# A convolution and a squared-ReLU MLP on one core: the first superblock of tokens in a set order, the biases moved to the second

## The chip, the cores and the metric

The kernel runs on one core of a Trainium2 chip. The metric is the device time of one execution in microseconds (us), as the median of several runs. Engines go by the profile's names: PE is TensorE, PEld its weight loads, DVE is VectorE, ACT is ScalarE, POOL is GpSimd, SP is SyncE, which here only issues DMAs.

## What is computed

Each of 8 sequences of 4096 tokens (192 channels) is convolved causally with 7 softmax-normalised taps per head. Then every token goes through an MLP of width 2048 with a squared ReLU:

```python
w = softmax(weight)                                  # 8 heads x 7 taps
out = np.einsum('hk,bskhg->bshg', w, x_unf)          # causal convolution
h = x @ w_in                                         # 192 -> 2048
r = np.maximum(h, 0.0)
g = s * (r * r) + b
return (g @ w_out).astype(np.float32)                # 2048 -> 192
```

The constant b contributes b times the column sums of w_out, one number for each output channel. That is the bias of which this document speaks.

## The kernel before, in words

**Tiling.** Everything is transposed: channels lie on the 128 partitions, tokens along the free axis. The 32768 tokens are 32 superblocks of 1024 (index n), each of two blocks of 512 (j = 0, 1). The 16 slices of the hidden width are taken as 8 pairs (p). One step (n, j, p) computes two slices of h for 512 tokens (`first`, 18 matmuls of 64 rows on L465, two at a time on the two halves of the array), squares them, and two steps later (LAG = 2) adds their share to the output accumulators (`second` on L529, or `second_whole` on L501 to L508 for n = 0). The numbers are kept as a high and a low part: qh and ql of the squares, W's two parts of the weights, sA and tB of the convolved tokens.

**Halves.** A matmul of 64 rows reads its tokens from either half of the partitions, so each of sA (channels 0 to 127) and tB (channels 128 to 191) has a copy with the halves exchanged, wA and wB. `swap` makes it with two DMAs on SP's queue (L156 and L157 of before). A step's matmuls read sA first, then tB and wB, then wA. The tB and wB of a superblock hold both of its blocks, in one tile each.

**Who does what in a step.** ACT: Relu of h out of PSUM (L474), the square (L475). DVE: the rounded copy qh (L481) and the remainder ql (L482). For n = 0 the copy qh is on ACT (L479).

**The next tokens.** While superblock n runs, DVE convolves superblock n+1. `Tokens.steps` is a generator, and each of its yields is one part: 7 taps for accA of block 0, 2 for splitting it, 7 taps for accB, 1 for hiB, 2 for the two halves of tB, 1 for the swap of tB into wB (it yields the mark "block 0"), then 9 for block 1 of accA: 29 parts. `convolve(k)` takes k parts behind DVE's last instruction. For n > 0 it is called with 2 at the pairs p < 7 of both blocks: 28 parts a superblock. `ready` calls `finish` ahead of a block's first step: `finish("block 0")` takes parts until it meets that mark; where the mark has already gone by, it meets none and takes all that is left.

**The weights.** They arrive as 64-bit floats. `Widen` makes the two parts of a pair's weights: an Abs on ACT (`magnitudes`), three DVE operations and two ACT copies into W (`top`), six DVE operations (`rest`, L288 to L295). In the first superblock, pair p+2 is widened while pair p runs; `column_sums` adds the weights up from step 8 on, and `biases` multiplies the sums by b on PE at the superblock's last pair.

**What sets the order.** Each engine executes in program order. `head()` pins its own order on four engines; behind it the order comes from a scheduler that takes what is ready by priority, with `issue_after` as the only hints. Superblock 0 goes by pairs, both blocks of a pair one after the other; the others go block by block.

Of the kernel before, what the change touches and what calls it, by code (L numbers as in the profile page):

```python
# [9 lines left out]
F32 = mybir.dt.float32  # L10
F32R = mybir.dt.float32r
# [12 lines left out]

CONV0, CONVN = 5, 2

SUM0 = 8

# [8 lines left out]
def conv_attention_then_squared_relu_mlp(  # L37
# [42 lines left out]

    @contextmanager
    def behind(*engines):


        with ExitStack() as stack:
            for e in engines:
                last = next(i for i in reversed(nc.cur_bb.bb.instructions) if i.engine == e.engine)
                stack.enter_context(tc.issue_after(last))
            yield

# [19 lines left out]
    class Tokens:  # L110
        def __init__(self, n):
            self.n = n
            self.sA, self.wA = {}, {}
            self.todo = self.steps() if n else iter(())

        def load(self):
# [54 lines left out]
        def split_B(self, acc):  # L171
# [13 lines left out]
            self.swap(self.wB, self.tB)  # L185

        def split_tensor(self, acc, hi):
# [58 lines left out]
    class Widen:  # L246
# [21 lines left out]
        def top(self):  # L268
            t, top = self.t, words[self.p][:, self.lo : self.hi, 1]
            nc.vector.tensor_scalar(  # L270
                t.bitcast(F32), t.bitcast(F32), TOP_MIN, TOP_MAX, op0=ALU.max, op1=ALU.min
            )
# [8 lines left out]
            for hi, _, t in self.parts(t.bitcast(F32)):  # L281
                nc.scalar.copy(hi, t)

        def rest(self):
# [12 lines left out]
        def all(self):  # L297
            self.magnitudes()
            self.top()
            self.rest()  # L300

# [40 lines left out]
    def head():  # L342
# [5 lines left out]
        for _ in range(WARM):  # L348
# [3 lines left out]
            )  # L352
        w0, w0out, w1 = Widen(0, 0, CI), Widen(0, CI, CT), Widen(1, 0, CT)

# [19 lines left out]
        next(split)  # L374
        w0.top()
        next(split)
        fetch(2)
        w0.rest()
        w0out.magnitudes()
        tB = one.tB = xs.tile([P, 2, BLK], F32R, name="tB")  # L380
# [6 lines left out]
        lo(tB[bottom, 0, :], top)  # L387
        lo(wB[top, 0, :], top)
        w0out.top()
        w1.magnitudes()  # L390
        w0out.rest()
        sA = one.sA[1] = xs.tile([P, 2, BLK], F32R, name="sA", bufs=3)
# [6 lines left out]
        one.swap(wB[:, 1, :], tB[:, 1, :])  # L399
        w1.top()  # L400
        w1.rest()

    ENGINES = (nc.vector, nc.scalar, nc.tensor, nc.sync)
    with in_order(*ENGINES):
        head()
    headed = {
        e: next(i for i in reversed(nc.cur_bb.bb.instructions) if i.engine == e.engine)
        for e in ENGINES
    }

    @contextmanager
    def behind_head(*engines):
        with ExitStack() as stack:
            for e in engines:
                stack.enter_context(tc.issue_after(headed[e]))
            yield

# [26 lines left out]

    bias = const.tile([P, 2], F32, name="bias")

    def biases():


        pb = ps_h.tile([P, 2, BLK], F32, name="h")[:, 0, 0:2]  # L450
        for i, cols in enumerate((sumA[:, 0, 0:P], sumB[:, 0:P])):
            nc.tensor.matmul(pb[:, i : i + 1], cols, bb, start=True, stop=True)
        nc.scalar.copy(bias, pb)


    def first(n, j, p):
# [12 lines left out]
        for at in (0, 2, 1):  # L469
            both(0, 1, at, at == 0, False)  # L470
            both(0, 2, at, False, False)
            both(1, 1, at, False, at == 1)
        q = act.tile([P, 2, BLK], F32, name="q")
        nc.scalar.activation(q, h, AF.Relu)  # L474
        nc.scalar.activation(q, q, AF.Square)  # L475
        qh = qs.tile([P, 2, BLK], F32R, name="qh")
        ql = qs.tile([P, 2, BLK], F32R, name="ql")
        if n == 0:
            nc.scalar.copy(qh, q)  # L479
        else:  # L480
            nc.vector.tensor_copy(qh, q)  # L481
        nc.vector.tensor_tensor(ql, q, qh.bitcast(F32), op=ALU.subtract)  # L482
# [9 lines left out]
    def second_whole(n, j, p, qh, ql):  # L492


        if (j, p) == (0, NPAIR - 1):
            biases()
        a1, a2 = accumulators(n, j, p)
# [11 lines left out]
        if p == NPAIR - 1:  # L509
            t0 = n * SUP + j * BLK  # L510
            oA = outs.tile([P, BLK], F32, name="oA")
            nc.scalar.activation(oA, a1, AF.Identity, scale=sb, bias=bias[:, 0:1])
            nc.sync.dma_start(outT[0:P, t0 : t0 + BLK], oA)
            oC = outs.tile([DB, BLK], F32, name="oC", bufs=1)
            nc.scalar.activation(oC, a2[DB:P, :], AF.Identity, scale=sb[DB:P], bias=bias[DB:P, 1:2])
            oB = outs.tile([P, BLK], F32, name="oB")
            nc.vector.scalar_tensor_tensor(
                oB[0:DB], a2[0:DB, :], sb[0:DB], oC, op0=ALU.mult, op1=ALU.add
            )
            nc.sync.dma_start(outT[P:D, t0 : t0 + BLK], oB[0:DB])  # L520
            del acc[n, j]
# [47 lines left out]
    def last(t0, accs):  # L569
# [7 lines left out]
        for k, o in ((1, oB), (3, oC)):  # L577
            nc.vector.scalar_tensor_tensor(
                o, accs[k][0:DB], sb[0:DB], o, op0=ALU.mult, op1=ALU.add
            )  # L580
        nc.gpsimd.tensor_tensor(oB, oB, oC, op=ALU.add)
        nc.sync.dma_start(outT[P:D, t0 : t0 + BLK], oB)
# [12 lines left out]


    steps = [(0, j, p) for p in range(NPAIR) for j in range(2)]
    START = len(steps)
    steps += [(n, j, p) for n in range(1, NSUP) for j in range(2) for p in range(NPAIR)]
    queue = []  # L600
# [3 lines left out]
    def convolve(k):  # L604

        done = object()
        with behind(nc.vector):
            while k and coming[0] in tok:
                if next(tok[coming[0]].todo, done) is done:
                    coming[0] += 1  # L610
                else:
                    k -= 1

    def upkeep(at, n, j, p):

        if n == 0 and j == 1 and p + 2 < NPAIR:
            with behind_head(*ENGINES):
                if p + 3 < NPAIR:
                    fetch(p + 3)
                Widen(p + 2, 0, CT).all()  # L620
                if p == 0:
                    start_tokens(1)
        if 0 <= at - SUM0 < NPAIR - 1:
            with behind(nc.vector):
                column_sums(at - SUM0 + 1)
        if n == 0:
            if at >= CONV0:
                convolve(CONVN)
        elif p < NPAIR - 1:
            if j == 0 and p == 0:  # L630
                with behind_head(nc.sync):
                    start_tokens(n + 1)
            convolve(2)

    def ready(n, j, p):
        if p == 0 and n > 0:
            tok[n].finish("block 0" if j == 0 else None)
        if n > 0 and j == 1 and p == 0:
            tok.pop(n - 1)

    for at in range(0, START, 2):
        batch = steps[at : at + 2]
        for step in batch:
            ready(*step)
        for k, step in enumerate(batch):
            with behind_head(nc.scalar, nc.tensor):
                queue.append((*step, *first(*step)))
            upkeep(at + k, *step)
        while len(queue) > LAG:
            second_whole(*queue.pop(0))  # L650
    for at, step in enumerate(steps[START:], START):
        ready(*step)
        queue.append((*step, *first(*step)))
        upkeep(at, *step)
# [42 lines left out]
```

## Time and profile before

| | us |
|---|---|
| median of 3 runs (lowest, highest) | 2316.5 (2315.3, 2318.49) |
| the profiled execution | 2314.63 |
| its span, first to last instruction | 2312.8 |
| PE busy / DVE / ACT / POOL | 2295.4 / 1754.7 / 1289.0 / 306.0 |

The profile page gives the busy time of each engine. The timeline view lists instructions as start, duration, engine, line, tiles and, in brackets, the idle time ahead and what ended it. The windows view sums a stretch: length, then the busy time and number of instructions of PE, PEld, DVE, ACT and POOL, the granted TensorE clock, the busy share of the DMA engines, GB/s. The issue view gives the time from a DMA's issue to its landing. A matmul of 512 columns is drawn 0.39 us long while the next starts 0.23 us behind it, so PE's busy time hides short pauses.

### The profile page before, as it was taken

To read this page: it belongs to the slowest core of one execution; us is meant where nothing else is said; L and a number is where in the kernel's file an instruction comes from. 1 tells how busy PE (TensorE), PEld (TensorE's weight loads), DVE (VectorE), ACT (ScalarE), POOL (GpSimd) and SP (SyncE) were. 2 spreads that over 40 slices of the span, in tenths; PEclk is the share of its full clock that TensorE was granted. 3 is DMA by queue.
4 is the path that set the end of the run, shared out by engine and by line. 5 is a ranking of instruction groups with operands and counts; after the bars stand their busy time and mean duration, and the time that the engine had idled before them with its cause. 6 is when DMAs were issued, how large, how long until landed. Compare 5 with 4: busy or idle time off the path is not lost.

```text
span 2312.8 us, 45113 instructions
## 1 busy us (share of the span) xinstructions
PE 2295.4 (99%) x19334; PEld 1829.4 (79%) x19334; DVE 1754.7 (76%) x1993; ACT 1289.0 (56%) x1408; POOL 306.0 (13%) x207
## 2 busy tenths in 40 slices
PE   8999999999999999999999999999999999999998
PEld 5688888888888888888888888888888888888887
DVE  8877777777777777777777777777777777777764
ACT  7755555555555555554555555555555555555554
POOL 0001011011110110111111101101111011011111
PEclk9999999999999999999999999999999999999999
DMA  5112121111111111111112111111112121111110
GB/s 174 55 33 60 37 60 51 52 42 44 54 51 51 42 52 46 54 55 50 46 42 56 51 51 42 49 49 51 51 43 59 38 60 52 51 42 41 43 38 17
DMA packets 46521, 117.77 MB, mean 51 GB/s; under 512 B 8240, under 2 KB 8496, under 8 KB 46320
## 3 DMA queue, kind: packets, MB, share of 16 engines
q1 hardware_dynamic: 45808, 114.49, 17.9%
q8 instruction: 151, 2.47, 0.5%
q10 hardware_dynamic: 512, 0.40, 0.1%
q14 instruction: 50, 0.41, 0.1%
HBM read 31.63 MB, written 25.17 MB: 25 GB/s over the span
## 4 chain that ended last, share of the span: by engine, by line
PE 78%; issue 16%; DVE 2%; POOL 2%; DMA 1%; ACT 1%; POOLq 0%; DVEq 0%; ACTq 0%
PE acc L529 40%; PE h L465 37%; POOL oB L559 1%; DMA oC<-oB 1%; POOL oC L565 1%; PE acc L218 1%; DVE ql L482 1%; DVE t L277 0%; DVE c L289 0%; DVE W L293 0%; ACT q L474 0%; DVE W L295 0%; PE acc L501 0%; ACT q L475 0%; DMA tap<-in_taps 0%
## 5 line engine op out<-in xcount | busy, mean ns | idle before, releaser
L474 ACT ACTIVATE q<-h 128x1024 f32<-128x1024 f32 x512 | 526.4, 1028 | 719.3 <-PE h L465 716.2
L481 DVE CAST qh<-q 128x1024 fp32r<-128x1024 f32 x496 | 373.3, 753 | 451.0 <-ACT q L475 447.5
L482 DVE TENSOR_TENSOR ql<-q,qh 128x1024 fp32r<-128x1024 f32 x512 | 654.5, 1278 | 60.1 <-ACT qh L479 6.6
L529 PE MATMUL acc<-qh,W 64*128 64x512 f32 x3968 | 623.3, 392 | 0.0
L475 ACT ACTIVATE q<-q 128x1024 f32<-128x1024 f32 x512 | 544.4, 1063 | 16.1
L465 PE MATMUL h<-sA,W 64*128 64x512 f32 x3072 | 442.7, 393 | 6.8 <-ACT q L474 6.8
L529 PEld LDWEIGHTS acc<-qh,W 64*128 64x128 f32 x3968 | 371.7, 184 | 91.2
L465 PE MATMUL h<-wA,W 64*128 64x512 f32 x3072 | 442.5, 392 | 0.0
L465 PE MATMUL h<-wB,W 64*128 64x512 f32 x1536 | 440.4, 392 | 1.9 <-DVE accA L148 1.9
L465 PE MATMUL h<-tB,W 64*128 64x512 f32 x1536 | 440.1, 392 | 0.0
L529 PE MATMUL acc<-qh,WB 64*128 64x512 f32 x1984 | 391.8, 392 | 0.0
L529 PE MATMUL acc<-ql,WB 64*128 64x512 f32 x1984 | 391.8, 392 | 0.0
L529 PE MATMUL acc<-ql,W 64*128 64x512 f32 x1984 | 391.8, 392 | 0.0
L465 PEld LDWEIGHTS h<-sA,W 64*128 64x128 f32 x3072 | 286.7, 184 | 81.4 <-ACT q L474 9.3
L148 DVE SCALAR_TENSOR_TENSOR accA<-xA,tap,accA 128x512 f32<-128x512 f32 x378 | 340.8, 902 | 6.8
L465 PEld LDWEIGHTS h<-wA,W 64*128 64x128 f32 x3072 | 288.8, 184 | 70.7
L465 PEld LDWEIGHTS h<-wB,W 64*128 64x128 f32 x1536 | 282.4, 184 | 49.6 <-DMA wB<-tB 2.8
L559 POOL TENSOR_TENSOR oB<-oB,oB 128x512 f32<-128x512 f32 x61 | 115.4, 1891 | 1486.9 <-ACT oB L558 1486.9
L465 PEld LDWEIGHTS h<-tB,W 64*128 64x128 f32 x1536 | 282.4, 184 | 24.0
L529 PEld LDWEIGHTS acc<-ql,WB 64*128 64x128 f32 x1984 | 185.9, 184 | 45.6
L529 PEld LDWEIGHTS acc<-ql,W 64*128 64x128 f32 x1984 | 185.8, 184 | 45.6
L529 PEld LDWEIGHTS acc<-qh,WB 64*128 64x128 f32 x1984 | 185.8, 184 | 45.6
(95 smaller groups left out, 1019.9 us busy)
## 6 DMA issues: line engine op xcount, KB each, us to landing
wA<-sA SPq DMA_DIRECT2D x128, 256.0 KB, 3.7
outT<-oA SPq DMA_DIRECT2D x63, 256.0 KB, 2.0
wB<-tB SPq DMA_DIRECT2D x62, 256.0 KB, 3.4
xA<-in_xT SPq DMA_DIRECT2D x24, 515.0 KB, 3.4
oC<-oB SPq DMA_DIRECT2D x61, 128.0 KB, 2.2
outT<-oC SPq DMA_DIRECT2D x61, 128.0 KB, 2.3
xB<-in_xT SPq DMA_DIRECT2D x56, 129.5 KB, 2.7
words<-in_w SPq DMA_DIRECT2D x7, 768.0 KB, 6.4
```

What stands on the lines that cost most here:

```text
L148: nc.vector.scalar_tensor_tensor(acc, src, w[:, k : k + 1], acc, op0=ALU.mult, op1=ALU.add)
L218: nc.tensor.matmul(acc, diag[:, k, :], x[:, k : k + BLK], start=k == 0, stop=k == K - 1)
L465: nc.tensor.matmul(h[:, i, :], w_in(w, p, chunk[0], rows), chunk[part], start=start, stop=stop)
L474: nc.scalar.activation(q, h, AF.Relu)
L475: nc.scalar.activation(q, q, AF.Square)
L481: nc.vector.tensor_copy(qh, q)
L482: nc.vector.tensor_tensor(ql, q, qh.bitcast(F32), op=ALU.subtract)
L529: nc.tensor.matmul(accs[to + 2 * i], w(f, r), q[r, f % 2, :], start=start, stop=stop)
L559: nc.gpsimd.tensor_tensor(o[1], o[1], o[3], op=ALU.add)
L565: nc.gpsimd.tensor_tensor(oC, oC, o[1][0:DB], op=ALU.add)
```

## The change

`head()` widens pair 1 before the output weights of pair 0 and leaves two steps, `his` and `rest`, to be called apart. Superblock 0 becomes a loop over `pair(p)` in which DVE, ACT and PE are pinned to the order of the code. The parts of superblock 1's convolution in each pair are a table, CONV: three numbers for three places in the pair. For n = 1 alone, ACT makes the copies of the accB split and writes block 0's wB itself, so that only block 1's wB needs a DMA. `finish` is written anew. `column_sums` and `biases` go to the pairs of (1, 0); the outputs of superblock 0 are made without the bias, and POOL adds it behind them. The very last output's sum moves from POOL to DVE.

```diff
-CONV0, CONVN = 5, 2
-SUM0 = 8
+CONV = ((0, 0, 0),) + ((0, 0, 1),) * 5 + ((0, 1, 3), (4, 2, 2))
...
+        def split_B_at_once(self, acc):
...
+            nc.scalar.copy(hiB, acc)
+            for j in range(2):
+                r = slice(j * DB, (j + 1) * DB)
+                places = (self.tB, self.wB) if j == 0 else (self.tB,)
+                for k, to in enumerate(places):
+                    nc.scalar.copy(to[k * DB :][0:DB, j, :], hiB[r, :].bitcast(F32))
+                for k, to in enumerate(places):
+                    nc.vector.tensor_tensor(
+                        to[(1 - k) * DB :][0:DB, j, :], acc[r, :], hiB[r, :].bitcast(F32),
+                        op=ALU.subtract,
+                    )
+                yield "block 0" if j == 0 else None
+            self.swap(self.wB[:, 1, :], self.tB[:, 1, :])
...
-                    yield from self.split_B(acc)
-                    yield "block 0"
+                    if self.n == 1:
+                        yield from self.split_B_at_once(acc)
+                    else:
+                        yield from self.split_B(acc)
+                        yield "block 0"
...
-        def finish(self, upto=None):
-            for at in self.todo:
-                if upto and at == upto:
-                    break
+        def part(self):
+
+            at = next(self.todo, False)
+            if at == "block 0":
+                self.begun = True
+            return at is not False
+
+        def finish(self, block):
+            while not (block == 0 and self.begun) and self.part():
+                pass
...
+        pb = ps_h.tile([P, 2, BLK], F32, name="h")
+        for k, cols in enumerate((sumA[:, 0, 0:P], sumB[:, 0:P])):
+            for i in range(2):
+                r = slice(i * HB, (i + 1) * HB)
+                nc.tensor.matmul(pb[:, i, k : k + 1], cols[r], bb[r], start=True, stop=True)
+        nc.scalar.copy(bias[:, 0:2], pb[:, 0, 0:2])
+        nc.vector.tensor_tensor(bias[:, 0:2], bias[:, 0:2], pb[:, 1, 0:2], op=ALU.add)
+        nc.vector.tensor_copy(bias[0:DB, 2:3], bias[DB:P, 1:2])
+        for o, to, k in unbiased:
+            rows = slice(0, o.shape[0])
+            nc.gpsimd.tensor_scalar(o, o, bias[rows, k : k + 1], None, op0=ALU.add)
+            nc.sync.dma_start(to, o)
...
-        nc.gpsimd.tensor_tensor(oB, oB, oC, op=ALU.add)
+        nc.vector.tensor_tensor(oB, oB, oC, op=ALU.add)
...
+    def pair(p):
+
+        ha, hb = first(0, 0, p), first(0, 1, p)
+        if 0 < p < NPAIR - 1:
+            wide[p + 1].rest()
+        convolve(CONV[p][0])
+        qa = squares(ha, nc.scalar.copy)
+        if p == 0:
+            wide[2].top()
+        elif p + 2 < NPAIR:
+            wide[p + 2].magnitudes()
+        queue.append((0, 0, p, *lows(*qa)))
+        if 0 < p and p + 2 < NPAIR:
+            wide[p + 2].top()
+        convolve(CONV[p][1])
+        qb = squares(hb, nc.scalar.copy)
+        if p + 2 < NPAIR:
+            wide[p + 2].his()
+        queue.append((0, 1, p, *lows(*qb)))
+        convolve(CONV[p][2])
+        while len(queue) > (LAG if p < NPAIR - 1 else LAG - 1):
+            second_whole(*queue.pop(0))
...
+    for n, j, p in steps:
+        if p == 0:
+            tok[n].finish(j)
...
+        if (n, j) == (1, 0):
+            if p < NPAIR - 1:
+                with behind(nc.vector):
+                    column_sums(p + 1)
+                convolve(2 - p % 2)
+            else:
+                biases()
         elif p < NPAIR - 1:
...
+            convolve(3 if n == 1 else 2)
```

The order of DVE in the first superblock, one pair of it. A line that ends in W_85 is a weight's last operation, ql is the remainder of a block's squares, accA the convolution of superblock 1. Before:

```order
L270 TENSOR_SCALAR t_740<-t_740 128x768
L274 TENSOR_SCALAR t_740<-t_740 128x768
L277 SCALAR_TENSOR_TENSOR t_740<-words_641,t_740 128x768
L482 TENSOR_TENSOR ql_512<-q_508,qh_511 128x1024
L148 SCALAR_TENSOR_TENSOR accA_466<-xA_301,tap_87,accA_466 128x512
L288 TENSOR_SCALAR c_747<-t_740 128x768
L148 SCALAR_TENSOR_TENSOR accA_466<-xA_301,tap_87,accA_466 128x512
L289 SCALAR_TENSOR_TENSOR c_747<-words_641,c_747 128x768
L148 SCALAR_TENSOR_TENSOR accA_466<-xA_301,tap_87,accA_466 128x512
L482 TENSOR_TENSOR ql_540<-q_536,qh_539 128x1024
```

And now, for one pair from its `rest` to its second ql:

```order
L325 TENSOR_SCALAR c_698<-t_623 128x768
L326 SCALAR_TENSOR_TENSOR c_698<-words_482,c_698 128x768
L330 TENSOR_TENSOR W_85<-t_623,W_85 128x640
L330 TENSOR_TENSOR WB_86<-t_623,WB_86 128x2x64
L332 TENSOR_TENSOR W_85<-W_85,c_698 128x640
L332 TENSOR_TENSOR WB_86<-WB_86,c_698 128x2x64
L518 TENSOR_TENSOR ql_712<-q_705,qh_708 128x1024
L305 TENSOR_SCALAR t_710<-t_710 128x768
L309 TENSOR_SCALAR t_710<-t_710 128x768
L312 SCALAR_TENSOR_TENSOR t_710<-words_571,t_710 128x768
L518 TENSOR_TENSOR ql_724<-q_717,qh_720 128x1024
L155 SCALAR_TENSOR_TENSOR accA_367<-xA_237,tap_87,accA_367 128x512
```

The taps, which lay between the parts of a weight, now lie once a pair behind the second ql.

The second place is DVE where tB of superblock 6 is made, late in superblock 5 (hiB is the rounded accB, and each row of tB is half a block's split). Before:

```order
L176 CAST hiB_4733<-accB_4493 128x512
L180 CAST tB_4731<-accB_4493 64x512
L181 TENSOR_TENSOR tB_4731<-accB_4493,hiB_4733 64x512
L481 CAST qh_4794<-q_4791 128x1024
L482 TENSOR_TENSOR ql_4795<-q_4791,qh_4794 128x1024
L180 CAST tB_4731<-accB_4493 64x512
L181 TENSOR_TENSOR tB_4731<-accB_4493,hiB_4733 64x512
L481 CAST qh_4824<-q_4821 128x1024
L482 TENSOR_TENSOR ql_4825<-q_4821,qh_4824 128x1024
L146 TENSOR_SCALAR accA_4828<-xA_4271,tap_87 128x512
```

Now:

```order
L183 CAST hiB_4946<-accB_4794 128x512
L513 CAST qh_4990<-q_4987 128x1024
L518 TENSOR_TENSOR ql_4992<-q_4987,qh_4990 128x1024
L187 CAST tB_4944<-accB_4794 64x512
L188 TENSOR_TENSOR tB_4944<-accB_4794,hiB_4946 64x512
L187 CAST tB_4944<-accB_4794 64x512
L188 TENSOR_TENSOR tB_4944<-accB_4794,hiB_4946 64x512
L513 CAST qh_5040<-q_5037 128x1024
L518 TENSOR_TENSOR ql_5042<-q_5037,qh_5040 128x1024
L513 CAST qh_5093<-q_5090 128x1024
```

Before, tB is done five blocks of squares ahead of superblock 6's first (qh and ql of the steps 3 to 7 of block 1 follow, the taps of block 1 between them). Now it follows the squares q_4987 of step (5, 1, 6); q_5037 are those of (5, 1, 7), and q_5090 already come from the h that reads this tB. On PE that h (h_5071) stands two steps behind the h of q_4987:

```order
L498 MATMUL h_5071<-sA_4727,W_85 128x512 x6
L498 MATMUL h_5071<-tB_4944,W_85 128x512
L498 MATMUL h_5071<-wB_4945,W_85 128x512 x2
L498 MATMUL h_5071<-tB_4944,W_85 128x512 x2
L498 MATMUL h_5071<-wB_4945,W_85 128x512
L498 MATMUL h_5071<-wA_4728,W_85 128x512 x6
```

PE's own order there is as before; what moved is DVE's making of tB, and with it the swap into wB_4945.

More of the change, by code (lines that the diff above doesn't have):

```diff
@@ L79, in conv_attention_then_squared_relu_mlp, with last_of, context @@
     ps_o = ctx.enter_context(tc.tile_pool(name="ps_o", bufs=2, space=bass.MemoryType.PSUM))
-    @contextmanager
-    def behind(*engines):
[L85 to L89, printed above, removed]
+    def last_of(*engines):
+        traced = nc.cur_bb.bb.instructions
+        last = [next(i for i in reversed(traced) if i.engine == e.engine) for e in engines]
+        @contextmanager
+        def context():
+            with ExitStack() as stack:
+                for i in last:
+                    stack.enter_context(tc.issue_after(i))
+                yield
+        return context
+    def behind(*engines):
+        return last_of(*engines)()
     @contextmanager
@@ L185, in split_B @@
             self.swap(self.wB, self.tB)
+        def split_B_at_once(self, acc):
+            self.tB = xs.tile([P, 2, BLK], F32R, name="tB")
+            self.wB = xs.tile([P, 2, BLK], F32R, name="wB")
+            hiB = xs.tile([P, BLK], F32R, name="hiB", bufs=1)
+            nc.scalar.copy(hiB, acc)
[11 more added lines that the diff above has]
+            self.swap(self.wB[:, 1, :], self.tB[:, 1, :])
         def split_tensor(self, acc, hi):
@@ L279, in top, with his @@
             )
-            for hi, _, t in self.parts(t.bitcast(F32)):
+        def his(self):
+            for hi, _, t in self.parts(self.t.bitcast(F32)):
                 nc.scalar.copy(hi, t)
@@ L295, in rest @@
                 nc.vector.tensor_tensor(lo, lo.bitcast(F32), f, op=ALU.add)
[L297 to L300, printed above, removed]
     w_words = weights64.bitcast(I32)
@@ L375, in head @@
         w0.top()
+        w0.his()
         next(split)
         fetch(2)
+        w1.magnitudes()
         w0.rest()
-        w0out.magnitudes()
+        w1.top()
         tB = one.tB = xs.tile([P, 2, BLK], F32R, name="tB")
@@ L388, in head @@
         lo(wB[top, 0, :], top)
+        w0out.magnitudes()
+        w1.his()
         w0out.top()
-        w1.magnitudes()
-        w0out.rest()
+        w1.rest()
         sA = one.sA[1] = xs.tile([P, 2, BLK], F32R, name="sA", bufs=3)
@@ L399, in head @@
         one.swap(wB[:, 1, :], tB[:, 1, :])
[L400 to L416, printed above, removed]
+        w0out.his()
+        w0out.rest()
+        wide[2].magnitudes()
+    wide = {p: Widen(p, 0, CT) for p in range(1, NPAIR)}
     sumA, sumB = None, None
@@ L443, in column_sums @@
             nc.vector.tensor_tensor(b[:, 0:DB], b[:, 0:DB], b[:, DB:P], op=ALU.add)
-    bias = const.tile([P, 2], F32, name="bias")
+    bias = const.tile([P, 3], F32, name="bias")
+    unbiased = []
     def biases():
[L450 to L453, printed above, removed]
+        pb = ps_h.tile([P, 2, BLK], F32, name="h")
[10 more added lines that the diff above has]
+            nc.sync.dma_start(to, o)
     def first(n, j, p):
@@ L472, in first, with squares @@
             both(1, 1, at, False, at == 1)
+        return h
+    def squares(h, cast):
         q = act.tile([P, 2, BLK], F32, name="q")
@@ L476, in first, with lows @@
         qh = qs.tile([P, 2, BLK], F32R, name="qh")
+        cast(qh, q)
+        return q, qh
+    def lows(q, qh):
         ql = qs.tile([P, 2, BLK], F32R, name="ql")
[L478 to L481, printed above, removed]
         nc.vector.tensor_tensor(ql, q, qh.bitcast(F32), op=ALU.subtract)
@@ L604, in convolve @@
     def convolve(k):
-        done = object()
         with behind(nc.vector):
             while k and coming[0] in tok:
-                if next(tok[coming[0]].todo, done) is done:
+                if tok[coming[0]].part():
+                    k -= 1
+                else:
                     coming[0] += 1
[L611 to L617, printed above, removed]
+    def pair(p):
[19 more added lines that the diff above has]
+            second_whole(*queue.pop(0))
@@ L618, in upkeep @@
+    with in_order(nc.vector, nc.scalar, nc.tensor):
+        with in_order(nc.sync):
+            head()
+        headed = last_of(nc.sync)
+        for p in range(NPAIR):
+            with headed():
                 if p + 3 < NPAIR:
                     fetch(p + 3)
-                Widen(p + 2, 0, CT).all()
                 if p == 0:
                     start_tokens(1)
[L623 to L628, printed above, removed]
-        elif p < NPAIR - 1:
[L630 to L654, printed above, removed]
+            pair(p)
+    begun = last_of(nc.vector, nc.scalar, nc.tensor)
+    steps = [(n, j, p) for n in range(1, NSUP) for j in range(2) for p in range(NPAIR)]
+    for n, j, p in steps:
+        if p == 0:
+            tok[n].finish(j)
+            if j == 0:
+                with headed():
+                    start_tokens(n + 1)
+            else:
+                tok.pop(n - 1)
+        with begun() if n == 1 else ExitStack():
+            h = first(n, j, p)
+            queue.append((n, j, p, *lows(*squares(h, nc.vector.tensor_copy))))
+        if (n, j) == (1, 0):
[3 more added lines that the diff above has]
+                convolve(2 - p % 2)
+            else:
+                biases()
+        elif p < NPAIR - 1:
+            convolve(3 if n == 1 else 2)
```

20 lines of the change are left out of this document (8 added, 12 removed).

## The prediction

> **What bounds the kernel now.** I read the page's busy times first, then the windows view for where PE has pauses, then PE's row of waits.
>
> ```profile
> span 2312.8 us, 45113 instructions
> PE 2295.4 (99%) x19334; PEld 1829.4 (79%) x19334; DVE 1754.7 (76%) x1993; ACT 1289.0 (56%) x1408; POOL 306.0 (13%) x207
> 0.00:100.00 100.00, 90.25 (x469) 60.64 (x469) 86.84 (x147) 74.59 (x102) 0.94 (x9) 0.98 0.35 108
> 400.00:1000.00 600.00, 600.00 (x5146) 481.69 (x5145) 457.94 (x508) 329.33 (x355) 82.09 (x55) 1.00 0.18 49
> PE h L465 <- ACT q L474: 6.8, 5, 2.1
> ```
>
> PE is the bound, and from 400 to 1000 us it never pauses: 30 of the 32 superblocks offer nothing to gain, and any wait that comes up there is paid in full, once for each superblock. What can be won lies in the first 116 us. So I work out two things: what the front gains, and whether the steady part still feeds PE.
>
> **The front.** These rows are PE's at the first wait, two waits of the pairs, an undisturbed pair, and the first `second` of superblock 1; then the swap that block (0, 1) needs and its time to landing.
>
> ```profile
> 22.38 0.39 PE L465 MATMUL h<-tB,W 64*128 64x512 f32 x1
> 58.19 0.97 PE L465 MATMUL h<-sA,W 64*128 64x512 f32 x6 [1.21 <-ACT q L474]
> 62.69 0.97 PE L465 MATMUL h<-sA,W 64*128 64x512 f32 x6 [2.13 <-ACT q L474]
> 71.36 0.97 PE L465 MATMUL h<-sA,W 64*128 64x512 f32 x6
> 80.63 0.97 PE L465 MATMUL h<-sA,W 64*128 64x512 f32 x6
> 116.31 0.39 PE L529 MATMUL acc<-qh,WB 64*128 64x512 f32 x2
> 22.00 1.05 SPq L157 DMA_DIRECT2D wB<-tB  x1
> wB<-tB SPq DMA_DIRECT2D x1, 128.0 KB, 3.5
> ```
>
> An undisturbed pair takes 80.63 - 71.36 = 9.27 us. (A step of a later superblock is 169.75 - 165.31 = 4.44 in the rows further down, 19 slots of 0.233: nine are a `first`, 2.10, and ten a `second`, 2.33.) In the changed order block (0, 1) is no longer interleaved with pair 1: behind the row at 22.38 it needs wB, which lands at 22.00 + 3.5 = 25.5. From there PE has six slots of 0.23 left (1.4), seven pairs' worth (7 x 9.27 = 64.9), and then two whole `second` (2 x 2.33), four `first` (4 x 2.10) and 0.4 for changes of row size (13.5): the first `second` of superblock 1 at 25.5 + 1.4 + 64.9 + 13.5 = 105.3 instead of 116.31, **11.0 us earlier**, if nothing else makes PE wait. Does it? Here are DVE's rows for one pair's weights, and two Relus that follow each other closely on ACT.
>
> ```profile
> 55.47 0.56 DVE L288 TENSOR_SCALAR c<-t 128x768 int32<-128x768 int32 x1
> 58.81 0.56 DVE L270 TENSOR_SCALAR t<-t 128x768 f32<-128x768 f32 x1
> 60.87 1.22 DVE L482 TENSOR_TENSOR ql<-q,qh 128x1024 fp32r<-128x1024 f32 x1
> 62.01 0.75 DVE L148 SCALAR_TENSOR_TENSOR accA<-xA,tap,accA 128x512 f32<-128x512 f32 x1
> 64.78 1.01 ACT L474 ACTIVATE q<-h 128x1024 f32<-128x1024 f32 x1
> 67.88 1.02 ACT L474 ACTIVATE q<-h 128x1024 f32<-128x1024 f32 x1
> ```
>
> A pair now costs DVE `rest` 58.81 - 55.47 = 3.34, `top` 2.06, two ql of 1.14 and a tap of 0.7: 8.4 us. ACT has two blocks of 67.88 - 64.78 = 3.10 and some 1.9 for Abs and copies: 8.1. Both stay under 9.27, and whatever ACT does ahead of a Relu waits for DVE work that the new order puts at least one ql earlier. So the waits for ACT at 58.19 and 62.69 go, and with them the lesser ones. The matmuls hide the widening; were DVE 0.9 us a pair slower, PE would wait by that much in each of six pairs.
>
> **The biases.** They are multiplied right behind h of (1, 0, 7), and DVE must have added up the weights by then.
>
> ```profile
> 95.53 1.23 DVE L482 TENSOR_TENSOR ql<-q,qh 128x1024 fp32r<-128x1024 f32 x1 [2.19 <-ACT qh L479]
> 98.36 0.22 DVE L443 TENSOR_TENSOR words<-words 128x64 f32<-128x64 f32 x1
> 102.65 0.61 PE L452 MATMUL h<-bb,words 128*128 128x1 f32 x4
> ```
>
> The last sums come behind ql of step (1, 0, 6), 98.58 - 95.53 = 3.05 us after its start. A step's ql starts 5.3 us behind its h (the rows of the steady part below), so the sums end 8.3 us behind h of (1, 0, 6). PE is there after one step and one `first`, 4.43 + 2.10 = 6.5. That is a wait of 1.8 at least. At most it is 3.1: ACT's copy of accA stands ahead of the Relu of (1, 0, 5) and waits for the last tap, which lies two ql further on. I take 2.8. Eight small matmuls cost about what the row at 102.65 shows, 0.5, and the swap of block 1's sA, which DVE starts behind the sums, makes PE wait about 1 more for wA. Together **4.3 us lost** (2 to 5). POOL's four bias additions are an operation that the trace lacks; this is the nearest row.
>
> ```profile
> 2307.99 1.26 POOL L581 TENSOR_TENSOR oB<-oB,oC 64x512 f32<-64x512 f32 x1 [24.71 <-DVE oC L578]
> ```
>
> Four of them take 5 us by that row, 8 at one and a half times it, and their output DMAs are done about when ACT wants the oB buffers again, two `second` and two `first` later (9 us), so I cost them at nothing; without that cover ACT's evacuation would be late by some 2 us, once. At the end the sum on DVE (about 0.7) replaces POOL's 1.26: **0.4 gained**. The front in all: -11.0 + 4.3 - 0.4 = **-7.1**.
>
> **The steady part, where `finish` decides.** Before, `finish("block 0")` ran past its mark and emptied the generator, so superblock n's 29 parts were all taken when it began, and the 28 parts of its steps went to superblock n+1 alone: tB was split and swapped in the middle of block 1. The new `finish(0)` stops once "block 0" has gone by. The 9 parts of block 1 stay behind and are taken out of the next 28. Counted through the code, superblock 2 begins with 22 of its parts taken, 3 with 21, 4 with 20, and 5 and all later ones with 19. Part 18 and 19 are the two halves of the tB split, part 20 its swap. So from superblock 5 on, the split is DVE's last convolution work, behind ql of step p = 6, and the swap follows it, as the order of DVE for superblock 6 shows. When can PE have it?
>
> ```profile
> 165.31 0.86 PE L465 MATMUL h<-sA,W 64*128 64x512 f32 x6
> 166.01 0.39 PE L465 MATMUL h<-wB,W 64*128 64x512 f32 x1
> 169.75 0.86 PE L465 MATMUL h<-sA,W 64*128 64x512 f32 x6
> 169.78 0.69 DVE L481 CAST qh<-q 128x1024 fp32r<-128x1024 f32 x1 [0.96 <-ACT q L475]
> 170.57 1.23 DVE L482 TENSOR_TENSOR ql<-q,qh 128x1024 fp32r<-128x1024 f32 x1
> 171.72 0.75 DVE L148 SCALAR_TENSOR_TENSOR accA<-xA,tap,accA 128x512 f32<-128x512 f32 x1
> 227.34 0.42 DVE L180 CAST tB<-accB 64x512 fp32r<-64x512 f32 x1
> 227.80 0.69 DVE L181 TENSOR_TENSOR tB<-accB,hiB 64x512 fp32r<-64x512 f32 x1
> 228.52 0.69 DVE L481 CAST qh<-q 128x1024 fp32r<-128x1024 f32 x1
> 227.80 0.46 SPq L157 DMA_DIRECT2D wB<-tB  x1
> 228.52 0.46 SPq L156 DMA_DIRECT2D wB<-tB  x1
> wB<-tB SPq DMA_DIRECT2D x1, 256.0 KB, 3.1
> wB<-tB SPq DMA_DIRECT2D x1, 256.0 KB, 3.5
> 102.22 0.50 PE L465 MATMUL h<-wB,W 64*128 64x512 f32 x1 [1.86 <-DVE accA L148]
> ```
>
> Let h of step p = 6 start at 0. Its qh starts at 169.78 - 165.31 = 4.47, ql at 5.26, and DVE is free for the next at 6.41. Cast, difference, cast, difference follow at 6.41, 6.87, 7.59 and 8.05; the casts are done at 8.01, the differences at 8.74. The two DMAs go out at 8.05 and 8.77 (as at 227.80 and 228.52) and land at 8.05 + 3.1 = 11.15 and 8.77 + 3.5 = 12.27. PE begins superblock n's first h two steps on, at 2 x 4.43 = 8.87, reaches wB 0.70 later, at 9.57, and needs the other half one slot later, at 9.80. So it waits 1.6 us, does one slot, and waits again until 12.3: **2.5 us late** in all. The trace of before has that very wait once, the row at 102.22: the second half of that tile was split a moment ahead of PE's need, too. Nothing catches up afterwards, since PE has no slack. Superblocks 5 to 31 are 27 x 2.5 = 67.5; superblock 4, whose first half is split a step earlier, pays 8.77 - 1.18 + 3.5 - 9.80 = 1.3. Together **+68.8**. With landings 0.2 quicker or slower it is 63 to 74.
>
> **What the clock makes of it** is the one open price.
>
> ```profile
> 22.89:26.30 3.41, 1.97 (x13) 1.35 (x15) 3.31 (x8) 3.32 (x4) 0.00 (x0) 1.00 0.85 236
> 60.43:63.85 3.42, 1.28 (x12) 0.98 (x12) 3.42 (x6) 2.83 (x5) 0.00 (x0) 1.00 0.00 0
> 63.85:67.26 3.41, 3.41 (x15) 2.27 (x12) 3.41 (x6) 3.35 (x4) 0.00 (x0) 0.50 0.00 0
> ```
>
> After the wait that ends at 62.69, the granted clock is 0.50 for exactly 3.41 us (63.85 to 67.26). It cost 1.6: from 62.69 to 71.36 are 8.67 us, for an undisturbed pair less one `first`, 9.27 - 2.2 = 7.07. In the stretch of the same length ahead of it PE was busy 1.28 us; the stretch with 1.97 us was followed by no drop. The new wait, where it lies wholly within such a stretch, leaves 1.4 to 1.5 us of PE busy, nearer to the one that dropped. So each of 27 entries may cost 1.6 more, 0 to 43 us in all. A stretch of 3.41 holds a wait of 2.5 wholly in about a quarter of its positions, but a superblock of 73.4 us is 21.5 stretches, so two positions are tried in turn, and one with a drop is 75.0 us, 22.0 stretches, so a drop tends to repeat. I take 13 drops, half: **+20.8**.
>
> The Trainium skill ("TensorE: Matmul & The Clock Gate", what is actually happening) says that PE falls back to half clock after at least one idle window of about 3.4 us. By that rule a wait of 2.5 us never drops the clock, and this term would be 0. The row at 60.43 shows a drop after a stretch in which PE worked for 1.28 us, so here the measurement decides, and the rule's result stays as a rival.
>
> **The sum.** The profiled execution took 2314.63 (span 2312.8 and 1.8 around it), 1.9 under the median of 2316.5. 2314.63 - 7.1 + 68.8 + 20.8 = 2397.1; on the median's footing **2399 us**, 3.6% slower.
>
> **Rivals.** (1) The clock never drops: 2316.5 - 7.1 + 68.8 = 2378. For it speaks the busy 1.97 us without a drop; against it the 1.28. (2) It drops at nearly every entry, since 22.0 stretches fit: 2378 + 27 x 1.6 = 2421. (3) The other side: the swap is covered, as it is in superblocks 2 and 3, and only the front is left: 2316.5 - 7.1 = 2309. It decides at 2.5 us: were the split behind ql of p = 5, 4.43 us earlier, both halves would land at 7.8, ahead of 9.57. Against it is the order of DVE, which has it behind q of p = 6, and PE's, two steps on.
>
> **How the numbers follow.** 13 drops, give or take 8: 0.38. No drops, or up to four: 0.33. Nearly all: 0.24. Covered: 0.04. The last 0.01 is no change, front and steady part even. The range takes in both clock ends with the bounds of the landings: 2370 to 2424. Faster by over 0.2% 0.04, within 0.2% (about what a measurement of this kernel can tell from no change) 0.01, slower 0.95.
>
> **What would show it.** PE's row of waits names h on DVE or on the DMA wB<-tB, with 54 waits of 0.7 to 1.6 us and some 60 us in all, one pair of them every 73 to 75 us from the fourth superblock on. The pairs of superblock 0 run at 9.27 from about 36 to 92 us without a wait, and a wait of 2 to 3 us stands ahead of the bias matmuls. The number of stretches at clock 0.50 tells the rivals apart: none leaves 2378. The prediction is wrong if superblocks keep to 71 us: then the parts are not where I counted them.

## The result, and the profile after

The changed kernel takes 2426.36 us (median of 4 runs, 2424.52 to 2427.25) against 2317.49 of the kernel before (4 runs, 2315.3 to 2318.59): a ratio of 1.047, 95% interval 1.0452 to 1.0488. It is slower by 109 us where 82 were forecast, and 2 us above the range.

The page of the profile after: span, busy times, and its share of the chain that ended last; then PE's row of waits (us in total, times, longest).

```profile
span 2424.1 us, 45116 instructions
PE 2357.5 (97%) x19338; PEld 1904.8 (79%) x19338; DVE 1727.0 (71%) x1994; ACT 1289.2 (53%) x1412; POOL 335.6 (14%) x210
PE h L498 <- DMA wB<-tB: 53.9, 58, 2.7
PE h L479 <- issue: 3.4, 1, 3.4
```

PE's busy share fell from 99% to 97%: it waits 58 times for the swap of tB, twice in each of the superblocks 4 to 31, once in superblock 2 and once in the front. The timeline shows one entry, that of superblock 5: DVE's ql of step p = 6, the last split of tB behind it and its DMA, then PE's first h, and PE's first sA matmul of the superblocks 6 and 31.

```profile
382.36 1.23 DVE L518 TENSOR_TENSOR ql<-q,qh 128x1024 fp32r<-128x1024 f32 x1
385.12 0.69 DVE L188 TENSOR_TENSOR tB<-accB,hiB 64x512 fp32r<-64x512 f32 x1
385.84 0.48 SPq L163 DMA_DIRECT2D wB<-tB  x1
385.97 0.87 PE L498 MATMUL h<-sA,W 64*128 64x512 f32 x6
386.68 0.39 PE L498 MATMUL h<-tB,W 64*128 64x512 f32 x1
388.29 0.50 PE L498 MATMUL h<-wB,W 64*128 64x512 f32 x1 [1.22 <-DMA wB<-tB]
389.39 0.50 PE L498 MATMUL h<-wB,W 64*128 64x512 f32 x1 [0.60 <-DMA wB<-tB]
461.04 0.86 PE L498 MATMUL h<-sA,W 64*128 64x512 f32 x6
2338.03 0.86 PE L498 MATMUL h<-sA,W 64*128 64x512 f32 x6
```

The swap's second DMA goes out at 385.84, when PE has all but begun the superblock, and lands with PE's last wait, at 389.39. One matmul pair is worked between the two waits. From start to start, less a slot of 0.23, they leave PE idle for 1.38 and 0.87 us, 2.25 together. From superblock 5 to 31 the entries are (2338.03 - 385.97) / 26 = 75.08 us apart, where before it was 70.93. A wait of 2.5 does not make 4.15. The windows view (length, then busy time of PE, PEld, DVE, ACT and POOL, the granted clock, DMA share, GB/s) shows the rest, at the first and the last of these entries:

```profile
386.79:390.20 3.41, 1.59 (x12) 0.86 (x10) 1.23 (x1) 0.00 (x0) 0.00 (x0) 1.00 0.44 114
390.20:393.62 3.42, 3.42 (x20) 2.71 (x18) 0.24 (x1) 2.08 (x2) 0.00 (x0) 0.51 0.02 5
2342.70:2346.11 3.41, 3.41 (x20) 2.67 (x18) 0.93 (x2) 2.08 (x2) 0.00 (x0) 0.50 0.00 0
core 0: 2424.1 us, clock 0.979
```

The clock is halved for 3.4 us behind each of these entries. From 390.20 to 2342.70 are 26 x 75.10 us, 22.0 stretches of 3.41 each time, and all 27 entries from superblock 5 on have the drop. The mean clock of 0.979 agrees: 2424.1 x 0.021 = 51 us under full speed are 30 stretches of 1.7, these 27, two of the front and the end.

### The profile page after: what moved, and what is told of

Read it like the earlier page. It is cut to its first block, busy times and chain, and to the rows that moved or that the text cites. A ratio compares the mean times of both kernels' runs of the same rounds, so it can differ in the third digit from the quotient of the medians.

```text
span 2424.1 us, 45116 instructions
## 1 busy us (share of the span) xinstructions
PE 2357.5 (97%) x19338; PEld 1904.8 (79%) x19338; DVE 1727.0 (71%) x1994; ACT 1289.2 (53%) x1412; POOL 335.6 (14%) x210
## 4 chain that ended last, share of the span: by engine, by line
PE 86%; DMA 4%; DVE 4%; ACT 3%; issue 2%; DVEq 0%; SPq 0%; ACTq 0%
PE acc L563 43%; PE h L498 41%; DMA wB<-tB 4%; DVE tB L188 2%; ACT q L511 1%; ACT q L510 1%; DVE tB L187 1%; DVE qh L513 1%; PE acc L247 1%; PE acc L535 0%; PE acc L536 0%; PE acc L540 0%; PE acc L541 0%; PE acc L542 0%; DVE ql L518 0%
## 5 line engine op out<-in xcount | busy, mean ns | idle before, releaser
L513 DVE CAST qh<-q 128x1024 fp32r<-128x1024 f32 x496 | 351.7, 709 | 605.5 <-ACT q L511 604.4
L518 DVE TENSOR_TENSOR ql<-q,qh 128x1024 fp32r<-128x1024 f32 x512 | 664.5, 1298 | 62.5 <-ACT qh L513 8.3
L563 PE MATMUL acc<-qh,W 64*128 64x512 f32 x3968 | 640.5, 399 | 0.0
L498 PE MATMUL h<-wB,W 64*128 64x512 f32 x1536 | 450.9, 397 | 53.9 <-DMA wB<-tB 53.9
L563 PEld LDWEIGHTS acc<-qh,W 64*128 64x128 f32 x3968 | 392.7, 190 | 87.6
L563 PE MATMUL acc<-qh,WB 64*128 64x512 f32 x1984 | 409.5, 405 | 0.0
L563 PE MATMUL acc<-ql,WB 64*128 64x512 f32 x1984 | 409.4, 405 | 0.0
L563 PE MATMUL acc<-ql,W 64*128 64x512 f32 x1984 | 400.8, 397 | 0.0
L563 PEld LDWEIGHTS acc<-ql,WB 64*128 64x128 f32 x1984 | 198.2, 192 | 44.0
L563 PEld LDWEIGHTS acc<-qh,WB 64*128 64x128 f32 x1984 | 197.3, 191 | 43.3
```

The source lines that it names most:

```text
L498: nc.tensor.matmul(h[:, i, :], w_in(w, p, chunk[0], rows), chunk[part], start=start, stop=stop)
L513: cast(qh, q)
L563: nc.tensor.matmul(accs[to + 2 * i], w(f, r), q[r, f % 2, :], start=start, stop=stop)
```

## The experiments

Times are medians; the ratio is that to the kernel before in runs on the same chip.

**The old finish in the changed kernel.** From superblock 2 on, `finish` empties the generator again where the mark has gone by.

```diff
-            while not (block == 0 and self.begun) and self.part():
+            stop = block == 0 and (self.n == 1 or not self.begun)
+            while not (stop and self.begun) and self.part():
                 pass
```

> The changed kernel, with the old emptying of a superblock's convolution at its start from superblock 2 on (finish stops at the mark of block 0 only if that mark has not gone by yet). Theory: all of the loss from superblock 4 on is the late swap of tB and the clock drop behind it, so every superblock is back at 70.93 us, no clock drop is left beside those at 25 and 131 us, and what remains is the front as the changed trace shows it (superblock 3 begins 2.5 us earlier than before): 2313 to 2315 us. Rival: if the steady part also pays for something else in the change (the order of the instructions, the taps' places), some of the 4.1 us a superblock stays and the time is above 2330.

Measured: 2314.55 us, ratio 0.9994 (0.9986 to 1.0003). The superblocks are back at 70.93 us from the third on, and the 112 us are gone; `finish` is where the loss came from.

**The new finish in the kernel before.** Only `finish` is exchanged, with a flag that `convolve` sets at the mark.

```diff
-            for at in self.todo:
-                if upto and at == upto:
-                    break
+            while not (upto and self.begun):
+                at = next(self.todo, False)
+                if at == "block 0":
+                    self.begun = True
+                if at is False:
+                    break
```

> The kernel before, with the new finish alone (it stops once the mark of block 0 has gone by). Counted through the code, superblock 2 begins with 21 of its parts, 3 with 20, 4 and later with 19: a wait of 1.2 us at superblock 3 and of 2.4 at each of 28 others. Theory: the drop of the clock comes with the wait, costs 1.7, and repeats, since 70.93 + 2.4 + 1.7 = 75.1 us are 22 of its stretches: 2317 + 1.2 + 28 x 4.1 = 2433, some 4 us less for each entry that passes before the first drop. Rival one, half of the entries drop (as predicted for the change): about 2409. Rival two, the drops come from the changed front or order, not from this wait: 2386.

Measured: 2433.73 us, ratio 1.0503 (1.0489 to 1.0517). The loss comes with the old front and the old order too, so it is `finish` alone. The windows view of this kernel at the entries of superblock 4 and 5, in stretches counted back from the drop at 395.6, shows how the drops begin:

```profile
317.14:320.56 3.42, 2.25 (x20) 1.49 (x16) 2.75 (x4) 1.10 (x2) 0.00 (x0) 1.00 0.59 143
320.56:323.97 3.41, 2.61 (x19) 1.93 (x21) 0.12 (x1) 0.65 (x1) 0.00 (x0) 1.00 0.05 13
395.59:399.01 3.42, 3.42 (x18) 2.67 (x18) 0.00 (x0) 1.26 (x2) 0.00 (x0) 0.51 0.02 5
```

Superblock 4 has a full wait and no drop: its two parts, 1.33 and 1.07 us of idleness, lie on either side of the stretch's end at 320.56. Superblock 5 has a drop at 395.59, and every one after it has one too. The profiled runs of two kernels, with waits in different places of a stretch, have 27 drops in a row each.

**Zeros in the wait.** Six pairs of matmuls by a tile of zeros, which add 0 to h, stand ahead of those that wait; in a second kernel two pairs.

```diff
         for at in (0, 2, 1):
+            if at == 2 and n >= 5 and (j, p) == (0, 0):
+                for _ in range(6):
+                    for i in range(2):
+                        chunk = halves[i][0]
+                        rows = slice(i * HB, (i + 1) * HB)
+                        nc.tensor.matmul(
+                            h[:, i, :], zero[rows, :], chunk[1], start=False, stop=False
+                        )
```

> The changed kernel, with six pairs of matmuls by a tile of zeros put between the matmuls by sA and those by tB in the first step of every superblock from the fifth on: they add 0 to h and take 6 x 0.233 = 1.4 us, about the first part of the wait. Theory: the time of the wait stays (the swap lands when it did), but PE is busy for half of it, the clock stays at 1.00, and each of 27 entries saves the 1.7 us of its drop: 2426 - 27 x 1.7 = 2380. Rival: the 1.7 us behind each wait is a cost of the wait or of the steps behind it and not of idleness: 2426 as before; or idleness of 0.9 us suffices for a drop: 2426 too, with the stretches at 0.50 still there.

> As the kernel with six pairs of zero matmuls in the wait, with two pairs instead: 0.47 us of it filled, 1.8 us left idle at each of 27 entries, where the changed kernel leaves 2.25 and drops at each, and the one with six leaves 0.9 and drops at one. Where the drop begins is open. If 1.8 us of idleness are too little, the time is that of the kernel with six, 2389; if they suffice and the drops repeat, it is the changed kernel's, 2426; if only some positions drop, between.

Measured: 2389.08 us with six pairs, ratio 1.0311 (1.0297 to 1.0325), and 2422.33 with two, 1.0461 (1.0441 to 1.0481). In the timeline of the kernel with six, superblock 6 and the start of 7:

```profile
462.44 0.86 PE L500 MATMUL h<-sA,W 64*128 64x512 f32 x6
463.14 1.56 PE L510 MATMUL h<-sA,zero 64*128 64x512 f32 x12
465.85 0.49 PE L500 MATMUL h<-wB,W 64*128 64x512 f32 x1 [0.60 <-DMA wB<-tB]
535.95 0.86 PE L500 MATMUL h<-sA,W 64*128 64x512 f32 x6
core 0: 2385.3 us, clock 0.997
```

More work for PE, and 37 us less: the superblock takes 535.95 - 462.44 = 73.51 us. That takes the two prices apart. A late swap costs 73.51 - 70.93 = 2.58, the clock 75.08 - 73.51 = 1.57. My expectation of 2380 was 9 too low: it took 1.7 for a drop, and one drop of the 27 stayed, at superblock 5, where the wait left 1.7 us idle instead of 0.9. That makes 27 x 1.7 - 26 x 1.57 = 5 of the 9, and some 0.8 for the longer wait; the rest is no more than the spread of the runs (2387.16 to 2391.18). With two pairs filled, each entry of the profiled run still has its drop; the windows at superblock 5, then the timeline at 6:

```profile
386.79:390.20 3.41, 2.07 (x14) 1.16 (x12) 1.14 (x1) 0.00 (x0) 0.00 (x0) 1.00 0.43 113
390.20:393.60 3.40, 3.40 (x20) 2.64 (x18) 0.41 (x1) 2.08 (x2) 0.00 (x0) 0.50 0.02 5
462.09 0.39 PE L500 MATMUL h<-tB,W 64*128 64x512 f32 x1
463.25 0.50 PE L500 MATMUL h<-wB,W 64*128 64x512 f32 x1 [0.78 <-DMA wB<-tB]
464.36 0.50 PE L500 MATMUL h<-wB,W 64*128 64x512 f32 x1 [0.61 <-DMA wB<-tB]
```

Counted from start to start, less a slot of 0.23, its two waits are 463.25 - 462.09 - 0.23 = 0.93 and 0.88, 1.8 us together. The profiled run, of 2426.32 us and a mean clock of 0.979, is one of two; the other took 2418.34 at 0.983, which by an estimate makes it some five drops fewer (8 / 1.57). By that, 1.8 us do not drop the clock at every entry of every run.

**One part more a superblock.** The other way to mend it: `convolve` takes 29 parts, as many as a superblock has.

```diff
-            convolve(3 if n == 1 else 2)
+            convolve(3 if n == 1 or (j, p) == (0, 0) else 2)
```

> The changed kernel with one part of the convolution more in the first step of each superblock: 29 parts a superblock, as many as there are, so each one keeps the lead of 22 with which superblock 2 begins. The swap of tB then follows step p = 5 instead of p = 6. Theory: it lands ahead of the need, no wait and no drop, 70.93 us a superblock, and the time is that of the kernel with the old finish within 2 us: 2313 to 2315. Rival: what counts is not the lead in parts but the leftover of block 1 being done inside the superblock, and the wait stays: above 2380.

Measured: 2312.73 us, ratio 0.9984 (0.9975 to 0.9993). The timeline at superblock 5 again: the second DMA of the swap, and PE's first h, which waits for nothing.

```profile
378.90 0.48 SPq L163 DMA_DIRECT2D wB<-tB  x1
384.52 0.86 PE L498 MATMUL h<-sA,W 64*128 64x512 f32 x6
385.23 0.62 PE L498 MATMUL h<-wB,W 64*128 64x512 f32 x2
```

**The lead held at 20.** The same extra part, but only from superblock 4 on (`n > 3 and (j, p) == (0, 0)`).

> The changed kernel with one part more in the first step of each superblock from the fourth on: the lead stays at 20, so the first half of tB is split behind ql of step p = 5 and the second half behind that of p = 6. Superblock 4 of the changed kernel shows what that costs once: a wait of 1.2 to 1.5 us and no drop of the clock. Theory: the price of an entry goes by the lead in parts, and a wait of 1.2 us is too short to drop the clock wherever it falls (72.4 us are 21.2 of the clock's stretches, so 28 entries try many positions): the kernel with 22 plus 28 x 1.5 = 2312.7 + 42 = 2355, with no stretch at 0.50 beside the three of the front and the end. Rival: any wait inside a stretch can drop the clock: some stretches at 0.50 and up to 28 x 1.5 more, 2398 at most.

Measured: 2357.43 us, ratio 1.0186 (1.0169 to 1.0202). An entry, and the mean clock:

```profile
387.00 0.39 PE L498 MATMUL h<-tB,W 64*128 64x512 f32 x1
387.55 0.50 PE L498 MATMUL h<-wB,W 64*128 64x512 f32 x1 [0.17 <-DMA wB<-tB]
388.67 0.50 PE L498 MATMUL h<-wB,W 64*128 64x512 f32 x1 [0.62 <-DMA wB<-tB]
core 0: 2355.6 us, clock 0.998
```

One part's lead is worth (2357.43 - 2312.73) / 28 = 1.6 us an entry, and 27 of the 28 entries of the profiled run, with waits like these two, 0.32 and 0.89 from start to start, 1.2 to 1.4 us together, drop no clock. The other one (superblock 17, at 1258.57) left 1.9 us idle, cut by the end of a stretch into 1.5 and 0.4, and has no drop either.

**What the second superblock still waits for.** The column sums of two pairs in the first step of (1, 0), so that the last sums come a step earlier; on top of one part more a superblock.

```diff
-                    column_sums(p + 1)
+                    for k in ((1, 2) if p == 0 else (p + 2,) if p < 6 else ()):
+                        column_sums(k)
```

> The kernel with one part more a superblock (2312.7), with the column sums of two pairs in the first step of (1, 0) and so the last sums one step earlier, at p = 5 instead of p = 6. Theory: the wait of 3.6 us ahead of the bias matmuls shrinks to about 1.2, but wA of block (1, 1), whose last part still lies behind ql of p = 6, is not landed sooner, and its wait grows from 0.9 to about 3: 2312 to 2314, no gain beyond a clock drop of 1.5. Rival: the biases are what the second superblock loses, and what is taken from their wait is gained: 2312.7 - 2.4 - 1.5 = 2309.

Measured: 2313.08 us, ratio 0.9986 (0.9977 to 0.9995), no change against 2312.73.

```profile
128.40 0.61 PE L479 MATMUL h<-bb,words 64*128 64x1 f32 x8 [0.81 <-issue]
134.30 0.50 PE L498 MATMUL h<-wA,W 64*128 64x512 f32 x1 [1.44 <-DMA wA<-sA]
135.43 0.73 PE L498 MATMUL h<-wA,W 64*128 64x512 f32 x4 [0.63 <-DMA wA<-sA]
```

The wait for the sums shrank from 3.4 us to 0.8, and wA, which had landed behind it unseen, became the next wait. (The 0.9 that my expectation gave to wA was superblock 2's wait for wB, a row of which stands below.) The profile's span is 1.1 us shorter, less than the runs can tell.

**All waits of the front together.** With that, two parts at every step of (1, 0), which issues wA's swap earlier; the bias matmuls behind the `second` of the last step; and in the head the swap of wB ahead of that of wA. No run tries these apart.

```diff
-                convolve(2 - p % 2)
-            else:
-                biases()
+                convolve(2)
...
             (second if item[0] else second_whole)(*item)
+        if (n, j, p) == (1, 0, NPAIR - 1):
+            biases()
...
+        nc.scalar.copy(tB[top, 1, :], hiB[bottom].bitcast(F32))
+        lo(tB[bottom, 1, :], bottom)
+        one.swap(wB[:, 1, :], tB[:, 1, :])
         sA = one.sA[1] = xs.tile([P, 2, BLK], F32R, name="sA", bufs=3)
...
         one.swap(wA, sA)
-        nc.scalar.copy(tB[top, 1, :], hiB[bottom].bitcast(F32))
-        lo(tB[bottom, 1, :], bottom)
-        one.swap(wB[:, 1, :], tB[:, 1, :])
```

> All that the front still waits for, taken away together: one part more a superblock, column sums a step earlier, two parts instead of one at the odd steps of (1, 0) (so wA's swap goes out two steps earlier), the bias matmuls behind the second of that step, and in the head the swap of wB ahead of that of wA. Theory: the wait of 2.7 us for wB at 22.4 becomes 1.3 and drops no clock, those of 3.6 and 0.9 in the second superblock go and so does their drop: 2312.7 - 1.4 - 4.5 - 2 x 1.5 gives 2304 at best, 2307 with a wait of some tenths left at each place; faster than the kernel before by 0.4% in either case. Rival: a new wait takes the place of those removed (the Relu or wA), and the time is 2311 to 2313.

Measured: 2305.97 us, ratio 0.9963 (0.9949 to 0.9977): the fastest of all, ahead of the kernel before by 10 us. In its timeline stand the first block's waits, the first `second`, the bias matmuls without a wait and the start of superblock 4, then its mean clock:

```profile
23.92 0.50 PE L498 MATMUL h<-wA,W 64*128 64x512 f32 x1 [0.31 <-DMA wA<-sA]
24.91 0.74 PE L498 MATMUL h<-wA,W 64*128 64x512 f32 x4 [0.49 <-DMA wA<-sA]
104.37 0.56 PE L563 MATMUL acc<-qh,WB 64*128 64x512 f32 x2
127.75 0.50 PE L479 MATMUL h<-bb,words 64*128 64x1 f32 x8
306.92 1.08 PE L498 MATMUL h<-sA,W 64*128 64x512 f32 x6
core 0: 2304.1 us, clock 1.000
```

The first `second` of superblock 1 comes at 104.37, 11.9 us earlier than before, and superblock 4 at 306.92, still 9.1 us earlier (316.05 before, in a row further down).

## Why the prediction was wrong: the drops of the clock

**The step that failed** is the count of the drops: a stretch "holds a wait of 2.5 wholly in about a quarter of its positions", so "I take 13 drops, half". All 27 entries dropped, a term of 27 x 1.57 = 42 us instead of 20.8. Two things were wrong in it. The wait need not lie wholly in one stretch: with two pairs filled some 1.8 us of idleness sufficed, so 0.45 of the 2.25 may fall outside at either end. By that estimate (3.41 - 2.5 + 2 x 0.45) / 3.41, about half of the positions serve instead of a quarter. With two positions half a stretch apart tried in turn (21.5 stretches), the first or second try should then hit, and it does: the first in the changed kernel, the second in the kernel before with the new finish. And the repetition, which I had worked out as 75.0 us or 22.0 stretches, is not a tendency: entries 75.08 us apart shift by 0.02 against 75.10, half a microsecond over all 27, so with the same wait the first hit decides those behind it. The numbers for rival 2 stood in the text, and I gave it 0.24 where they called for the most. The top of the range did not follow from its parts either: rival 2's 2421 with the slower landings (74 instead of 68.8) is 2426, not 2424.

**The wait itself was right.** 2.5 us from landings of 3.1 and 3.5, measured 2.58, in the superblocks that were counted and from the parts that were counted; superblock 4 at its lower price (72.47 - 70.93 = 1.5 for the 1.3 of the forecast). The Trainium skill ("TensorE: Matmul & The Clock Gate", what is actually happening) names at least one idle window of about 3.4 us as what brings half clock. If an idle window is one without work, the runs here contradict it as the first trace did: the stretch from 386.79 holds 12 matmuls, and the next is at half clock.

**The front was 4.2 us short of the 11.0 - 4.3 = 6.7 that I reckoned up to superblock 4.** These rows are from the changed kernel: the wait for wB and the stretch behind it, the first `second` of superblock 1, the sums' last ql and their end, the bias matmuls and the stretch behind them, a wait of superblock 2, and the start of superblock 4, in it and (L465) before.

```profile
25.58 0.80 PE L498 MATMUL h<-wB,W 64*128 64x512 f32 x2 [2.74 <-DMA wB<-tB]
25.00:28.43 3.43, 2.85 (x14) 2.30 (x16) 1.61 (x2) 1.11 (x2) 0.00 (x0) 0.50 0.87 315
107.02 0.39 PE L563 MATMUL acc<-qh,WB 64*128 64x512 f32 x2
127.68 1.22 DVE L518 TENSOR_TENSOR ql<-q,qh 128x1024 fp32r<-128x1024 f32 x1 [0.48 <-PE h L498]
130.50 0.22 DVE L466 TENSOR_TENSOR words<-words 128x64 f32<-128x64 f32 x1
130.69 0.92 PE L479 MATMUL h<-bb,words 64*128 64x1 f32 x8 [3.44 <-issue]
130.80:134.22 3.42, 3.42 (x22) 3.22 (x24) 2.62 (x6) 1.12 (x2) 2.13 (x2) 0.50 0.47 101
172.46 0.49 PE L498 MATMUL h<-wB,W 64*128 64x512 f32 x1 [0.75 <-DMA wB<-tB]
313.50 0.86 PE L498 MATMUL h<-sA,W 64*128 64x512 f32 x6
316.05 0.86 PE L465 MATMUL h<-sA,W 64*128 64x512 f32 x6
```

The first `second` came 9.3 us earlier instead of 11.0: wB landed as reckoned, but the wait for it, of 2.7 us, dropped the clock once, which I had not priced there. By superblock 4 only 316.05 - 313.50 = 2.55 was left, so 6.8 were lost on the way instead of 4.3: 3.4 of waiting for the sums (I took 2.8 of at most 3.1), the eight matmuls, a second drop of 1.6, and 0.7 of waiting in superblock 2, which I had called covered; some 0.5 of the 6.8 has no name. The wait for wA that I added, about 1, did not show: the wait for the sums hid it, as the kernel with the earlier sums brought to light. The pairs ran at their pace without waiting for ACT, as forecast.

**The end** gained nothing. These are the first rows of the last evacuation on ACT, before and in the kernel with one part more:

```profile
2305.69 0.78 ACT L573 ACTIVATE oB<-acc,bias,sb 64x512 f32<-64x512 f32 x1 [3.52 <-PE acc L529]
2303.24 0.78 ACT L607 ACTIVATE oB<-acc,bias,sb 64x512 f32<-64x512 f32 x1 [3.53 <-PE acc L563]
```

To the end of the span are 2312.8 - 2305.69 = 7.1 us before and 2310.8 - 2303.24 = 7.6 now. The forecast looked at oB alone. Before, oB's last packets landed behind oA's (2311.19 against 2310.21); now oA's come last (2309.34, oB's at 2308.65). On DVE the sum stands ahead of oA's last operation, which starts 2306.09 - 2303.24 = 2.85 us behind the row above, where before it was 2307.83 - 2305.69 = 2.14. No run tried it apart.

**The sum** of what was found: -2.5 up to superblock 4, 1.5 there, 27 x (2.58 + 1.57) = 112.1 and some 0.4 at the end are 111.5; the spans differ by 2424.1 - 2312.8 = 111.3.

## What to carry to other kernels

Where work for the next stage is handed out in a fixed number of pieces a step, the number must be no less than what a stage needs: with 28 of 29 the lead shrinks by one a stage until something is late, and then it is late in every stage. When a wait recurs with a fixed period, work out that period in stretches of the clock before giving chances to its drops: near a whole number one hit can mean all. And before a wait is taken away, look at what lands just behind it.

## What was not expected of the hardware

A stretch of 3.41 us need not be idle, nor nearly so, for the next to run at half clock. Two waits of 0.9 us, with a pair of matmuls between, did it at 27 entries of 27 in the profiled run of the kernel with two zero pairs; waits that add up to 1.2 to 1.4 us did it at none of 27 (the lead held at 20). Where the boundary lies is open. PE's busy time as it is drawn does not give it: the stretch with 2.07 us of it (two zero pairs) was followed by a drop, that with 1.97 from 22.89 on in the kernel before was not. Idleness alone does not give it either. One entry of the kernel with six zero pairs dropped after 1.7 us, while the kernel before with the new finish has a stretch in its first superblock with 1.9 us of idleness, counted in the same way (PE's wait for ACT that ends at 64.91), and the next one is at full clock:

```profile
61.14:64.56 3.42, 1.62 (x14) 0.96 (x12) 3.35 (x5) 2.71 (x4) 0.00 (x0) 1.00 0.00 0
64.56:67.97 3.41, 3.06 (x21) 2.28 (x22) 3.41 (x6) 3.38 (x5) 0.00 (x0) 1.00 0.00 0
```

Matmuls by zeros kept the clock up at 26 of 27 entries, and made a kernel 37 us faster that did more.
